# Batch 1 of the attention on the plan of batches 2 and 3, weight preparation and y's first block ahead of the second MoE

## Chip, cores and metric

The kernel runs on one core of one Trainium2 chip. The metric is the device time of one execution in microseconds (us), smaller is better.

## What is computed

```python
def _attn_ref(q, k, v, M_prev, z_prev, beta):      # B, H, S, D = 4, 8, 576, 64
    scores = scale * np.matmul(q, k.transpose(0, 1, 3, 2))
    scores = np.where(causal, -1000000000.0, scores)
    a = np.exp(scores - scores.max(-1, keepdims=True))
    a /= a.sum(-1, keepdims=True) + 1e-09
    local = np.matmul(a, v)
    mem_ret = np.einsum('bhsd,bhde->bhse', phi(q), M_prev)
    mem_norm = np.einsum('bhsd,bhd->bhs', phi(q), z_prev)[..., None] + 1e-06
    return g * mem_ret / mem_norm + (1 - g) * local

def _moe_ref(x, w_in, w_out):                      # 2304 tokens, 512 -> 2048 -> 512
    h = x @ w_in
    return (h * sigmoid(h)) @ w_out

def _moe2_ref(x, w_gate, w_val, w_out):            # 2304 tokens, 512 -> 1536 -> 512
    g = x @ w_gate
    return (g * sigmoid(g) * (x @ w_val)) @ w_out
```

The output is the second MoE of the first MoE of the attention, all in float32 (the weights of the MoEs come as float64 and are decoded on the chip).

## The kernel before, in words

Three stages follow each other. Attention and the first MoE overlap: the first MoE is cut into 256 groups of 12 matmuls (`moe1`, line 766), and the main loop at line 1203 puts attention slots between the groups. The second MoE, 36 rounds of gate and value products with the output products of earlier rounds between them, comes after.

**Precision.** A matmul on plain float32 data costs TensorE more than one on data rounded to a shorter form (`F32R`). Most operands are therefore split into a rounded high part and a rounded rest: a cast on ScalarE and a subtraction on VectorE or GpSimd, and three products (high by high, high by rest, rest by high).

**Attention** goes by units, one unit for each pair of heads (`unit`, line 306). A unit is a list of stages written as a string: `opF` for batch 1 and `opG` for batches 2 and 3 (batch 0 has two strings of its own). A "+" starts a new slot, and the next pair starts eight slots later. The two plans differ in the scores of the four 128-row blocks (`s_blk`, line 420): plan F multiplies q and k as plain float32 on 64 rows of the array for each head (line 437), plan G first splits both (`stack`, line 370: the casts of line 376, the subtractions of line 377) and makes three rounded products per head and block (line 441). Plan G also scales four of its nine attention tiles on ScalarE instead of GpSimd (line 485 GpSimd, line 489 ScalarE), and keeps one buffer for most tiles where plan F keeps two. At the start of batch 2 `open_G` closes F's tile pool and opens G's, and all slots of batch 1 end before those of batch 2 begin.

**Weights of the second MoE.** `prep_w2` (line 909) is a generator of 60 steps, 5 for each of 12 tiles of the hidden width. Each tile takes three 512 KB loads `raw` (gate, value, output: line 669 or 674), each decoded by one ScalarE and three VectorE instructions (lines 683 to 686), sums and differences for a seven-product scheme on GpSimd (lines 946 to 949), casts on ScalarE and subtractions on GpSimd (line 936), and stores to DRAM (`wg`, `wo`, line 917). It starts in `open_G`. While attention slots are left, every fifth group takes a step. Then `open_w2` (line 1016) finishes the tile under way, reloads the finished output weights from DRAM into SBUF (line 1031), and takes a step every fifth group until 24 groups are left. Then it brings in y's first block. What is left of the 60 steps is taken in the second MoE, up to three in each of its first rounds.

**y.** The first MoE's result is stored to DRAM (`yd`). `y_prep` (line 976) loads a block of 768 tokens as `ytop` and `ybot`, 768 KB each, and makes seven pieces of it, each split by a cast on ScalarE (line 993) and a subtraction on GpSimd (line 994); four of the pieces need a sum or difference first (lines 1000, 1003, 1007, 1011, VectorE). There are three blocks; twelve rounds of the second MoE use one.

**Second MoE.** A round (`up`, line 1089) makes seven products of six matmuls of 384 columns each, and between them the output products of earlier rounds (`down`, line 1165: nine matmuls of 512 columns for a tile). The last step before `down` is `pl` on GpSimd (line 1159). In this stage TensorE's order is as written; a scheduler orders all other engines, and TensorE in the first two stages. All engines execute in order, and nearly all DMAs are issued from SP's queue, also in order.

Of the kernel before, what the change touches and what calls it, by code (L numbers as in the profile page):

```python
# [25 lines left out]
    ps_m=3,  # L26
    ps_a=5,
    whi='v',
    stackb=2,
    rows=1,  # L30
    pA=0,
    sA=1,
# [18 lines left out]
    blks=1,  # L51
    pw=3,
    pt=4,
    every=5,
    late=5,
    y0=24,
    jit=3,
    G=dict(sc='ppppaaaap'),
    p_ring=15,
    pp=4,  # L60
# [31 lines left out]
def kernel(  # L92
# [15 lines left out]
    nc = tc.nc  # L108
# [69 lines left out]
    def open_at(name):  # L178
        if "x" in cur:
            cur["x"].close()  # L180
        cur["x"] = ExitStack()
        cur["pool"] = cur["x"].enter_context(tc.tile_pool(name=name, bufs=1, side="right"))
        cur["bufs"] = CFG["bufs" + name[2:]]
        cur["s4"] = [cur["pool"].tile([P, 640], F32, name=f"s4{i}") for i in range(CFG["n_s4"][name[2:]])]
        for x in cur["s4"]:
            nc.vector.memset(x[:, 576:640], 0.0)

    def open_F():
        kept.close()
        mx2.append(ph1.enter_context(tc.tile_pool(name="mx2", bufs=1)))  # L190
        open_at("atF")

    def open_G():
        open_at("atG")
        cur["pw"] = cur["x"].enter_context(tc.tile_pool(name="pw", bufs=1, side="right"))
        ph2["prep"] = prep_w2()
# [433 lines left out]
    for u, key in enumerate(units):  # L630
        step, stages = unit(u)
        if u == NP:
            stages.insert(0, lambda: open_at("atB"))
            at_slot = max(slots) + 1
        if u == 2 * NP:
            stages.insert(0, open_F)
            at_slot = max(slots) + 1
        if u == NP * CFG["stackb"] + NP:
            stages.insert(0, open_G)
            at_slot = max(slots) + 1  # L640
        for i, st in enumerate(stages):
            slots.setdefault(at_slot + i, []).append(st)
        for sup in key[2]:
            ready[key[0], sup] = at_slot + len(stages)
        at_slot += step
# [45 lines left out]
    def r_(ap):  # L691
        return ap.bitcast(F32R)
# [286 lines left out]
    def y_prep(i):  # L979
        top = ph2["yst"].tile([P, 2, T2], F32, tag="top", name="ytop")  # L980
        bot = ph2["yst"].tile([P, 2, T2], F32, tag="bot", name="ybot")
        t = ph2["yst"].tile([P, 2, HT], F32, tag="t", name="yt")
        for n, x in enumerate((top, bot)):
            nc.sync.dma_start(
                out=x, in_=yd[2 * P * n:2 * P * (n + 1), T2 * i:T2 * i + T2].rearrange("(k p) n -> p k n", p=P)
            )
        ys[i] = {}

        def put(nm, src):
            slot = (7 * i + YQ.index(nm)) % 10  # L990
            pool = ph2["yq" if slot < 7 else "ysp"]
            y = pool.tile([P, 2, 2, HT], F32, tag=f"y{slot}", name="y" + nm, bufs=1)
            nc.scalar.copy(r_(y[:, 0]), src)
            nc.gpsimd.tensor_sub(r_(y[:, 1]), src, y[:, 0])  # L994
            ys[i][nm] = r_(y)

        t0, t1, b0, b1 = top[:, :, 0:HT], top[:, :, HT:T2], bot[:, :, 0:HT], bot[:, :, HT:T2]
        yield
        put("B11", t0)
        nc.vector.tensor_sub(t, t1, t0)  # L1000
        put("T1", t)
        yield
        nc.vector.tensor_sub(t0, b1, t)
        put("T2", t0)
        yield
        put("B21", b0)
        nc.vector.tensor_sub(t1, b1, t1)
        put("T3", t1)
        yield
        put("B22", b1)  # L1010
        nc.vector.tensor_sub(t, b0, t0)
        put("T4", t)
        yield

    def open_w2():
        yield from drain()
        cur["x"].close()
        pha.close()
        ph2["wo"] = ctx.enter_context(tc.tile_pool(name="wo", bufs=1, side="right"))
        ph2["g"] = ctx.enter_context(tc.tile_pool(name="ps_g", bufs=1, space=PSUM, side="right"))  # L1020
        kept_o = list(wdo)
        x = open_prep("2", "right")
        n = 0
        while left() > CFG["y0"]:
            n += 1
            if n % CFG["late"] == 0:
                next(ph2["prep"])
            elif kept_o and n > 4:
                j = kept_o.pop(0)
                wos[j] = ph2["wo"].tile([P, 4, 256], F32, name=f"wo{j}")  # L1030
                nc.sync.dma_start(out=wos[j], in_=wdo[j])
            yield
        yield from drain()
        assert not kept_o
        x.close()
        ph2["yq"] = ctx.enter_context(tc.tile_pool(name="yq", bufs=1, side="right"))
        open_yst()
        for _ in y_prep(0):
            yield
# [143 lines left out]
    if True:  # L1183
# [16 lines left out]
        for kind, val in items:  # L1200
# [7 lines left out]
            else:  # L1208
# [10 lines left out]
                    attn_slot(slot)  # L1219
                    slot += 1  # L1220
                if slot < NSLOT:
                    if "prep" in ph2 and n_g % every == 0:
                        next(ph2["prep"], None)
                else:
                    if "late" not in ph2:
                        ph2["late"] = open_w2()
                    next(ph2["late"], None)
# [73 lines left out]
```

## Time and profile before

| what | us |
|---|---|
| median of 2 runs (lowest, highest) | 1141.92 (1141.29, 1142.55) |
| the profiled execution, device time | 1141.5 |
| its span | 1139.7 |
| TensorE busy in the span | 1097.1 (96%) |
| VectorE, ScalarE, GpSimd busy | 592.1, 519.0, 502.7 |

The span is what the profile covers; 1.8 us of the device time lie around it. Busy TensorE time is of pipelined matmuls with modelled ends, so a busy share near 100% says that TensorE hardly waited. The granted clock is TensorE's, as a share of 2.4 GHz; 0.5 is 1.2 GHz.

### The profile page before, as it was taken

How to read it: one execution, taken by the hardware profiler on the slowest of the kernel's cores; microseconds unless marked ns; L12 is line 12 of the kernel's file. 1: busy time of each engine (PE TensorE's matmuls, PEld its weight loads, DVE VectorE, ACT ScalarE, POOL GpSimd, SP SyncE). 2: the span in 40 equal slices, each digit the busy share in tenths (PEclk: the TensorE clock that was granted, in tenths of full speed). 3: DMA queues.
4: the chain of work that ended last, by engine and by line, in shares of the span. 5: the costliest groups of instructions: out<-in, count | busy, mean ns of one | idle time of the engine just before them, and what ended most of it. 6: DMA issues, size and time to landing. Idle time of an engine off the chain costs nothing.

```text
span 1139.7 us, 19219 instructions
## 1 busy us (share of the span) xinstructions
PE 1097.1 (96%) x6867; PEld 976.7 (86%) x6867; DVE 592.1 (52%) x1389; ACT 519.0 (46%) x1237; POOL 502.7 (44%) x562
## 2 busy tenths in 40 slices
PE   6899999999999999999999898799999999999998
PEld 4576877889898889989899897688989999999986
DVE  7996777765556555355635463653353333333320
ACT  6754766456555646465644343422342323323222
POOL 4675575456525426354445576641351113211123
PEclk8989999999999999999999998899999999999999
DMA  8975755455755626574449886885664645555501
GB/s 217 295 220 175 242 174 168 149 182 185 251 160 171 193 71 211 179 248 129 151 148 399 311 298 223 294 287 177 195 237 140 192 152 175 173 175 176 169 27 55
DMA packets 154479, 221.47 MB, mean 194 GB/s; under 512 B 75536, under 2 KB 108304, under 8 KB 154384
## 3 DMA queue, kind: packets, MB, share of 16 engines
q1 hardware_dynamic: 152208, 219.86, 58.7%
q8 instruction: 54, 0.88, 0.3%
q10 hardware_dynamic: 2176, 0.40, 0.2%
q14 instruction: 41, 0.34, 0.1%
HBM read 168.31 MB, written 51.90 MB: 193 GB/s over the span
## 4 chain that ended last, share of the span: by engine, by line
PE 77%; DVE 7%; POOL 5%; DMA 5%; issue 4%; ACT 2%; ACTq 0%; SPq 0%; POOLq 0%; DVEq 0%
PE y L867 16%; PE h L808 15%; PE po L1173 12%; PE gb L1104 8%; PE ga L1104 6%; PE U L576 4%; PE pst L327 3%; PE gd L1104 3%; PE gc L1104 3%; PE pss L441 2%; PE pss L437 2%; PE psm L399 1%; PE pss L471 1%; DMA raw<-in_moe_w_val_dram 1%; DVE raw L685 1%
## 5 line engine op out<-in xcount | busy, mean ns | idle before, releaser
L1159 POOL TENSOR_TENSOR pl<-r,ph 128x384 fp32r<-128x384 f32 x72 | 74.8, 1048 | 278.3 <-ACT ph L1158 217.1
L867 PE MATMUL y<-gh,w 128*128 128x320 f32 (+1 forms) x1024 | 174.9, 307 | 3.7 <-ACT gh L200 2.9
L818 POOL TENSOR_TENSOR gl<-th,gh 128x256 fp32r<-128x256 f32 (+1 forms) x128 | 110.5, 867 | 141.5 <-ACT gh L200 95.5
L808 PE MATMUL h<-xh,w 128*128 128x320 f32 (+1 forms) x1024 | 170.8, 304 | 1.2 <-ACT xh L200 0.5
L867 PEld LDWEIGHTS y<-gh,w 128*128 128x128 f32 x1024 | 147.5, 193 | 18.2 <-issue 9.3
L808 PEld LDWEIGHTS h<-xh,w 128*128 128x128 f32 x1024 | 144.6, 190 | 12.5 <-issue 7.2
L1104 PE MATMUL gb<-yT,w 128*128 128x384 f32 x648 | 134.6, 343 | 8.6 <-POOL yT L994 3.2
L1173 PE MATMUL po<-wo,ph 128*128 128x512 f32 x432 | 134.6, 397 | 3.4 <-ACT ot L1179 2.3
L1104 PEld LDWEIGHTS gb<-yT,w 128*128 128x128 f32 x648 | 118.2, 191 | 19.9 <-DVE e L1139 3.7
L816 DVE SCALAR_TENSOR_TENSOR th<-th,h 128x256 f32<-128x256 f32 (+1 forms) x128 | 57.1, 449 | 104.2 <-ACT th L815 104.0
L485 POOL TENSOR_TENSOR s<-s,r 128x128 f32<-128x128 f32 (+4 forms) x112 | 85.7, 794 | 46.4 <-DVE r L497 24.4
L1131 DVE TENSOR_TENSOR gd<-gb,e 128x384 f32<-128x384 f32 x36 | 20.4, 566 | 146.4 <-PE gb L1104 141.4
L867 PE MATMUL y<-gl,w 128*128 128x320 f32 (+1 forms) x512 | 96.0, 303 | 0.0
L808 PE MATMUL h<-xl,w 128*128 128x320 f32 (+1 forms) x512 | 93.0, 299 | 0.0
L1104 PE MATMUL ga<-yB,w 128*128 128x384 f32 x432 | 90.0, 345 | 0.6 <-issue 0.6
L1173 PEld LDWEIGHTS po<-wo,ph 128*128 128x128 f32 x432 | 79.2, 188 | 12.9 <-ACT ot L1179 3.2
L1173 PE MATMUL po<-wo,pl 128*128 128x512 f32 x216 | 85.2, 402 | 4.9 <-POOL pl L1159 4.9
L452 ACT ACTIVATE s<-s,mn 128x128 f32<-128x128 f32 (+3 forms) x128 | 71.1, 556 | 28.8 <-DVE mn L448 27.9
L1104 PEld LDWEIGHTS ga<-yB,w 128*128 128x128 f32 x432 | 79.2, 193 | 2.9 <-issue 0.9
L867 PEld LDWEIGHTS y<-gl,w 128*128 128x128 f32 x512 | 77.9, 193 | 3.1 <-issue 2.3
L815 ACT ACTIVATE th<-h 128x256 f32<-128x256 f32 (+1 forms) x128 | 51.7, 407 | 59.4 <-PE h L808 50.0
L808 PEld LDWEIGHTS h<-xl,w 128*128 128x128 f32 x512 | 76.0, 189 | 3.1 <-issue 2.4
(145 smaller groups left out, 1952.6 us busy)
## 6 DMA issues: line engine op xcount, KB each, us to landing
w<-wg SPq DMA_DIRECT2D x108, 512.0 KB, 4.3
w<-wd SPq DMA_DIRECT2D x80, 512.0 KB, 4.4
wg<-wo SPq DMA_DIRECT2D x36, 512.0 KB, 3.6
wd<-w SPq DMA_DIRECT2D x32, 512.0 KB, 3.9
raw<-in_moe_w_out_dram SPq DMA_DIRECT2D x28, 512.0 KB, 4.4
w<-wg SPq DMA_DIRECT2D x36, 256.0 KB, 3.3
raw<-in_moe_w_in_dram SPq DMA_DIRECT2D x16, 512.0 KB, 5.2
wo<-wo SPq DMA_DIRECT2D x14, 512.0 KB, 6.4
```

Source lines behind the costliest of these rows:

```text
L327: nc.tensor.matmul(dst, src, ident[0:n, 0:n], start=start, stop=True, is_transpose=True, skip_group_check=True)
L452: nc.scalar.activation(out=a, in_=a, func=ACTF.Exp, scale=-1.0, bias=mn, accum_out=o["sm", sup][:, col:col + 1])
L485: nc.gpsimd.tensor_mul(a, a, r.to_broadcast([P, w]))
L576: nc.tensor.matmul(U[64 * hh:64 * hh + 64, c0:c1], row_of("v", c)[:, hh], a(hh), start=False, stop=(m == len(todo) - 1), skip_group_check= ...
L808: nc.tensor.matmul(ps[:, :nt], w[:, kk, :], x[:, kk, :nt], start=(m == 0), stop=(m == 3 * KD - 1))
L815: nc.scalar.activation(out=th[:, :nt], in_=ps[:, :nt], func=ACTF.Tanh, scale=0.5 / WS)
L816: nc.vector.scalar_tensor_tensor(th[:, :nt], th[:, :nt], 1.0, ps[:, :nt], ALU.add, ALU.mult)
L818: tt(CFG["gl" if n >= CFG["n0"] else "gl0"]).tensor_sub(gl[:, :nt], th[:, :nt], f(gh[:, :nt]))
L867: nc.tensor.matmul(ps[:, :nt], w[:, c], g[:, :nt], start=(m == 0), stop=(m == last))
L1104: nc.tensor.matmul(dst, ws[nw][wi][:, P * kk:P * kk + P], y[ny][:, yi, kk], start=(start and m == 0), stop=(stop and m == 5), skip_group_c ...
L1159: nc.gpsimd.tensor_sub(pl, r, f(ph))
L1173: nc.tensor.matmul(po[t], a[:, c], w, start=(j == 0 and n == 0), stop=(j == F2 - 1 and n == 2))
```

## The change

Batch 1 takes plan G (`stackb=1`); G's pool is opened where F's was, so that no pool is changed between batches 1 and 2. The weight preparation exists from there on, but takes its first step at group 50 (`n_prep`), then every third group instead of every fifth, and every fourth group in `open_w2`. The reloads of the output weights take every second group. y's first block is prepared 32 groups before the end of the first MoE instead of 24, and the subtraction of y's pieces is on VectorE instead of GpSimd. In the second MoE's first rounds at most one step of preparation is taken.

```diff
@@ CFG
-    stackb=2,
+    stackb=1,
+    n_prep=50,
...
-    every=5,
-    late=5,
-    y0=24,
-    jit=3,
+    every=3,
+    late=4,
+    y0=32,
+    jit=1,
@@ def open_F():
         mx2.append(ph1.enter_context(tc.tile_pool(name="mx2", bufs=1)))
-        open_at("atF")
+        if CFG["stackb"] > 1:
+            open_at("atF")
+        else:
+            open_G()
@@ units
-        if u == NP * CFG["stackb"] + NP:
+        if CFG["stackb"] > 1 and u == NP * CFG["stackb"] + NP:
             stages.insert(0, open_G)
@@ def put(nm, src):
             nc.scalar.copy(r_(y[:, 0]), src)
-            nc.gpsimd.tensor_sub(r_(y[:, 1]), src, y[:, 0])
+            nc.vector.tensor_sub(r_(y[:, 1]), src, y[:, 0])
@@ def open_w2():
                 next(ph2["prep"])
-            elif kept_o and n > 4:
+            elif kept_o and n > 3 and n % 2 == 1:
@@ main loop
-                    if "prep" in ph2 and n_g % every == 0:
+                    if "prep" in ph2 and n_g >= CFG["n_prep"] and n_g % every == 0:
```

Lines of the changed kernel are four higher than those of before from `open_F` on.

On GpSimd at the start of the second MoE (`gl` is the last work of the first MoE, `yB` and `yT` are pieces of y, `raw` and `wo` belong to the weight preparation, `pl` to the second MoE) before:

```order
L818 TENSOR_TENSOR gl<-th,gh 128x320 x3
L994 TENSOR_TENSOR yB_8803<-ytop,yB_8803 128x768
L994 TENSOR_TENSOR yT_8807<-yt,yT_8807 128x768
L994 TENSOR_TENSOR yB_8854<-ybot,yB_8854 128x768
L994 TENSOR_TENSOR yT_8858<-ytop,yT_8858 128x768
L994 TENSOR_TENSOR yB_8881<-ybot,yB_8881 128x768
L994 TENSOR_TENSOR yT_8831<-ytop,yT_8831 128x768
L994 TENSOR_TENSOR yT_8885<-yt,yT_8885 128x768
L667 COPY raw_9176<-r 128x1
L667 COPY raw_9184<-r 128x1
L667 COPY raw_9187<-r 128x1
L1159 TENSOR_TENSOR pl<-r,ph 128x384
```

The same place now:

```order
L940 TENSOR_TENSOR wo<-t_8562,wo 128x2x256
L822 TENSOR_TENSOR gl<-th,gh 128x256 x3
L822 TENSOR_TENSOR gl<-th,gh 128x320 x4
L822 TENSOR_TENSOR gl<-th,gh 128x256 x4
L822 TENSOR_TENSOR gl<-th,gh 128x320 x4
L1163 TENSOR_TENSOR pl<-r,ph 128x384 x72
```

The seven subtractions for y's first block have left GpSimd, the last preparation stands 15 `gl` earlier, and nothing but `pl` follows to the end.

On VectorE in the last 32 groups of the first MoE (`th` and `yp` are the first MoE's two kinds of work there) now (before, `th`, `yp`, weight decoding and the four sums and differences of y's block stood there, but no `yB` or `yT`):

```order
L820 SCALAR_TENSOR_TENSOR th<-th,h 128x320 x2
L876 SCALAR_TENSOR_TENSOR yp<-y,yp 128x256 x2
L998 TENSOR_TENSOR yB_8759<-ytop,yB_8759 128x768
L876 SCALAR_TENSOR_TENSOR yp<-y,yp 128x256
L998 TENSOR_TENSOR yT_8763<-yt,yT_8763 128x768
L1007 TENSOR_TENSOR ytop<-ybot,yt 128x2x384
L998 TENSOR_TENSOR yB_8812<-ybot,yB_8812 128x768
L876 SCALAR_TENSOR_TENSOR yp<-y,yp 128x256
L998 TENSOR_TENSOR yT_8816<-ytop,yT_8816 128x768
L998 TENSOR_TENSOR yB_8833<-ybot,yB_8833 128x768
L1015 TENSOR_TENSOR yt<-ybot,ytop 128x768
L998 TENSOR_TENSOR yT_8787<-ytop,yT_8787 128x768
```

Between the last `yp` of these rows and the next `th` VectorE now has three subtractions of y's pieces and a difference to do; a `th` and a `yp` used to follow each other there.

On SP's queue where the attention has ended (`wo` with two numbers is a reload of output weights, `wo<-wo` with one a store, `raw` a load for the preparation) before:

```order
L674 DMA raw_7890<-in_moe_w_out_dram 128x1024
L712 DMA w<-wd_2_245 128x1024
L1031 DMA wo_7907<-wo_3732 128x1024
L1031 DMA wo_7932<-wo_4629 128x1024
L1031 DMA wo_7956<-wo_5567 128x1024
L712 DMA w<-wd_3_316 128x1024
L917 DMA wo_7773<-wo 128x1024
L1031 DMA wo_7980<-wo_6150 128x1024
L1031 DMA wo_8026<-wo_7075 128x1024
L1031 DMA wo_8044<-wo_7636 128x1024
L712 DMA w<-wd_4_372 128x1024
L712 DMA w<-wd_5_428 128x1024
```

And now:

```order
L1035 DMA wo_8295<-wo_6078 128x1024
L1035 DMA wo_8335<-wo_6461 128x1024
L1035 DMA wo_8373<-wo_7003 128x1024
L880 DMA yd<-yp 128x320
L1035 DMA wo_8428<-wo_7708 128x1024
L1035 DMA wo_8466<-wo_7952 128x1024
L880 DMA yd<-yp 128x320
L988 DMA ytop<-yd 128x2x768
L988 DMA ybot<-yd 128x2x768
L880 DMA yd<-yp 128x320
L673 DMA raw_8045<-in_moe_w_gate_dram 128x4x256
L673 DMA raw_8053<-in_moe_w_val_dram 128x4x256
```

Ten reloads stand together now (five more are ahead of these rows) with the loads of y's first block and of the next three `raw` right behind them; before there were seven (six in these rows), with the first MoE's own weights `w` between them, and y's loads right behind the seventh.

## Rows read from the trace of the kernel before

**Rows 1.** The page, chain that ended last, shares of the span by engine.

```profile
PE 77%; DVE 7%; POOL 5%; DMA 5%; issue 4%; ACT 2%; ACTq 0%; SPq 0%; POOLq 0%; DVEq 0%
```

**Rows 2.** Windows by stage: length, busy time of each engine (instructions), granted clock, DMA.

```profile
117.00:236.00 119.00, 119.00 (x785) 96.08 (x785) 89.18 (x247) 72.42 (x189) 70.32 (x78) 1.00 0.57 185
236.00:262.00 26.00, 24.15 (x177) 22.28 (x175) 16.39 (x37) 14.42 (x37) 16.18 (x19) 0.93 0.55 166
262.00:600.00 338.00, 337.45 (x2493) 304.79 (x2494) 182.87 (x518) 186.74 (x475) 156.48 (x206) 1.00 0.54 176
600.00:640.00 40.00, 37.10 (x262) 36.66 (x261) 18.34 (x32) 15.73 (x35) 20.73 (x22) 0.96 0.97 375
...
691.50:770.00 78.50, 64.55 (x311) 58.74 (x312) 43.63 (x61) 26.48 (x50) 43.79 (x37) 0.91 0.79 276
...
818.00:854.00 36.00, 33.83 (x167) 30.68 (x166) 18.87 (x22) 16.05 (x30) 23.74 (x15) 0.95 0.68 224
854.00:1110.00 256.00, 256.00 (x1330) 237.85 (x1328) 85.52 (x132) 73.45 (x148) 51.69 (x48) 1.00 0.48 154
```

**Rows 3.** Chain in order of time: start, length, what; rounds of the second MoE.

```profile
779.19 1.04 PE ga L1104 x6
...
788.63 1.04 PE ga L1104 x6
...
854.15 1.07 PE ga L1104 x6
...
865.72 1.07 PE ga L1104 x6
```

**Rows 4.** TensorE timeline after the first MoE: start, length, form, idle before.

```profile
690.74 0.75 PE L867 MATMUL y<-gl,w 128*128 128x320 f32 x4
...
695.46 0.97 PE L1104 MATMUL gb<-yT,w 128*128 128x384 f32 x4 [0.83 <-ACT gb L1128]
699.67 1.01 PE L1104 MATMUL gb<-yT,w 128*128 128x384 f32 x2 [3.23 <-POOL yT L994]
...
725.49 0.80 PE L1173 MATMUL po<-wo,pl 128*128 128x512 f32 x1 [2.73 <-POOL pl L1159]
...
766.98 1.31 PE L1104 MATMUL gb<-yT,w 128*128 128x384 f32 x6 [2.33 <-DVE e L1139]
```

**Rows 5.** Windows, plain float32 scores of batch 1 alone (line 437).

```profile
117.00:236.00 119.00, 21.76 (x64) 7.90 (x64) 1.00 0.57 185
```

**Rows 6.** Windows, rounded scores of batches 2 and 3 alone (line 441).

```profile
236.00:600.00 364.00, 31.16 (x192) 18.76 (x192) 1.00 0.54 176
```

**Rows 7.** Timeline, TensorE at the first scores of batch 2.

```profile
255.96 0.33 PE L441 MATMUL pss<-Kl,Qh 64*128 64x128 f32 x2 [1.85 <-POOL Kl L377]
```

**Rows 8.** Windows, the decoding of raw weights alone (line 683, one per load).

```profile
236.00:600.00 364.00, 14.15 (x21) 1.00 0.54 176
...
691.50:770.00 78.50, 3.92 (x6) 0.91 0.79 276
```

**Rows 9.** Timeline after the reloads of output weights, TensorE.

```profile
632.05 1.18 PE L867 MATMUL y<-gh,w 128*128 128x320 f32 x5 [2.88 <-ACT gh L200]
```

**Rows 10.** Lines by form: VectorE and GpSimd on two operands in SBUF.

```profile
L818 POOL TENSOR_TENSOR gl<-th,gh 128x320 fp32r<-128x320 f32 x64 | 59.1, 927 | 80.7 <-ACT gh L200 62.3 <-PE y L867 17.5 <-POOL q L202 0.5
...
L994 POOL TENSOR_TENSOR yT<-yt,yT 128x768 fp32r<-128x768 f32 x6 | 11.8, 1968 | 0.0
...
L1003 DVE TENSOR_TENSOR ytop<-ybot,yt 128x768 f32<-128x768 f32 x3 | 6.9, 2304 | 0.8 <-POOL yB L994 0.8
...
L1007 DVE TENSOR_TENSOR ytop<-ybot,ytop 128x768 f32<-128x768 f32 x3 | 3.8, 1258 | 1.1 <-DMA ybot<-yd 1.1
```

**Rows 11.** Line 1149, VectorE: shortest, median, longest in ns.

```profile
L1149 DVE SCALAR_TENSOR_TENSOR r<-sg,e x36: 549/1354/2187, 707.3 to 1105.4; 128x384 f32<-128x384 f32 x36
```

**Rows 12.** Chain in order of time, from first to second block of y.

```profile
823.19 6.37 DMA ytop<-yd
...
832.75 6.59 DMA out_dram<-ot
```

## The prediction

> **What bounds the kernel now.** I read the page's chain first: 77% of it is TensorE [rows 1], so a microsecond counts where TensorE waits, runs at the lower clock, or is spared a matmul. Then the busy time by stage [rows 2], where two columns matter: TensorE's busy time against the length of the stretch, and the granted clock. The granted clock has two levels, 1.0 (2.4 GHz) and 0.5 (1.2 GHz); a mean of 0.91 over 78.5 us means that work of 0.09 x 78.5 = 7.1 us was not done. Attention with the first MoE from 262 to 600 us is full (337.45 of 338 us, clock 1.00), and so is the second MoE after 854 us. The losses stand elsewhere: 1.85 + 1.8 us at the change of pools (236 to 262), 2.9 + 1.6 us after the end of attention (600 to 640), 14.0 + 7.1 us at the start of the second MoE (691.5 to 770), 2.2 + 1.8 us where it goes to y's second block (818 to 854) [rows 2].
>
> The second MoE can be measured more sharply by its rounds. Undisturbed, a round with y's first block takes 788.63 - 779.19 = 9.44 us, a later one 865.72 - 854.15 = 11.57 us [rows 3]; the first of all has no output products, so seven products of 1.04 us, 7.3 us. The first MoE's last matmuls end at 690.74 + 0.75 = 691.5 us [rows 4], and round 3 of the second block begins at 854.15 us: 162.7 us for 7.3 + 11 x 9.44 + 2 x 11.57 = 134.3 us of rounds. So 28.4 us are lost there. The TensorE timeline with its idle times names the causes [rows 4]: 3.23 us for GpSimd's split of y's first block, 2.73 us for `pl`, which stands behind the weight preparation on GpSimd, 2.33 us for VectorE's `e`, which stands behind the sums of y's second block, and two short waits of the 0.83 us kind on a ScalarE copy.
>
> **The change part by part.** The sum is made against the profiled execution, 1141.5 us, 0.4 us under the median of 1141.92.
>
> Scores of batch 1. The plain scores of four units keep TensorE busy for 21.76 us, 5.4 us a unit [rows 5]; the rounded ones of eight units 31.16 us, 3.9 us a unit [rows 6]. Four units save up to 6.2 us. Part of each busy time is the modelled end of a group, under which the next matmul already runs, so I take 5.0, and 3.5 as the other end. TensorE is full in batch 1 (the 21.76 us lie in a stretch with no idle time), so the saving counts. The two casts, two subtractions and the scaling that goes to ScalarE lie beside it: ScalarE and VectorE had 72.4 and 89.2 busy us in 119. **-5.0** (-6.2 to -3.5).
>
> Change of pools. The 3.7 us of 236 to 262 us hang on the empty pipeline that the new pool begins with: TensorE waited 1.85 us for the first `Kl` [rows 7]. Without the barrier between batches 1 and 2 this goes; a first `Kl` is now waited for at the start of batch 1, where GpSimd has no preparation in its queue. **-2.5** (-3.7 to 0).
>
> Start of the second MoE. All 36 raw loads (12 tiles by 3) now come before it; 6 were decoded in it [rows 8]. With them go the GpSimd queue in front of `pl`, the raw loads between the weight loads on SP, and the sums of y's second block in front of `e`, since the order brings these ahead of the stage. What is late next is the ScalarE copy (two waits, 1.4 us) and the step to y's second block, 4.0 us, with 0.5 us for the rest: 28.4 - 5.9 = 22.5 go. The bounds: nothing of the 5.9 stays, or 12 us of new waits do. **-22.5** (-28 to -11).
>
> The step to y's second block. The wait there is a chain of transfers: `ytop` for the third block lands 6.37 us after it could be issued, and an output store behind it took 6.59 us, on which `ot`'s two buffers hang [rows 12]. The order keeps store and loads in the same places. VectorE now carries four more subtractions there, in front of `gd`: **+1** (-4 to +3).
>
> Denser preparation. The attention stretch decodes 21 loads now [rows 8]; the order puts about six more into it, and all 30 come at three groups a step instead of five. Cover: VectorE is busy 182.9 us of 338, ScalarE 186.7, GpSimd 156.5 [rows 2]. By that stretch a load costs TensorE nothing; by the second MoE, where six cost some 12 us, 2 us each. I stay near the first, as it is the same stage: **+2** (0 to +12).
>
> Reloads of output weights. Ten instead of seven, then y's loads, then three raw loads: the ScalarE decode that waits for the first of these holds `th` and `gh` behind it, and TensorE waits for those, as it did for 2.88 us [rows 9]. The transfers grow by three of 512 KB, but no weights of the first MoE stand between them: **0** (-4.5, all that was lost, to +6).
>
> y's first block on VectorE. Between the `yp` and the `th` of its last groups VectorE gets seven subtractions and two differences. A subtraction of two SBUF operands of 768 took 1.26 us beside an idle GpSimd, 2.30 beside a busy one [rows 10], so nine take 11 to 21 us, with two `yp` more. TensorE has about eight groups of work ahead, 12 us. **+3** (0 to +9).
>
> The sum: -5.0 - 2.5 - 22.5 + 1 + 2 + 0 + 3 = -24.0; 1141.5 - 24.0 = 1117.5, and 0.4 for the median: 1118 us.
>
> On the subtractions the trace shows that VectorE's `r` from two SBUF operands takes 0.549 us at best and 2.187 at worst [rows 11], while nothing but GpSimd's load differs. The Trainium skill, page "SBUF — State Buffer", section "SBUF: two separate sides", says that VectorE with two SBUF inputs and GpSimd take a shared port pair by an exclusive lock, the later one waiting for the whole instruction. By that rule the move helps in the second MoE and hurts in the first, and the trace's long `r` agrees; what it would cost here is the second rival, worked out from rows.
>
> **The rivals.** The forecast, gains of 18 to 30 us, has 0.50.
>
> More comes free: the step to y's second block, reached with GpSimd idle, loses nothing (-4), the reloads spread by two groups cost nothing (-4.5): 1118 - 8.5 = 1109 us. For it: four subtractions of 1.97 us [rows 10] leave GpSimd's queue in front of `pl`. Against: the transfers of rows 12 stay. 0.14.
>
> The lock in the first MoE's tail: each of the seven subtractions waits for a `gl` of 0.93 us [rows 10], 6.5 us, and each `gl` for a subtraction, so that the tail loses 9 instead of 3 us: 1124 us. For it: rows 11. Against: TensorE's lead of eight groups. 0.15.
>
> The gain is handed back in the first MoE: the ten reloads hold the decode and cost 6 us more, preparation 6 instead of 2: 1128 us. For it: rows 9. Against: the full stretch in rows 2. 0.16.
>
> Slower: preparation every third group puts 30 loads into the attention stretch at a pace at which ScalarE, VectorE and GpSimd, all in order, hand each wait for a raw load on to TensorE. Without the +2 the sum is -26, so it decides from 26/30 = 0.87 us a load on; at 1.0 us the time is 1146 us. For it: 2 us a load in the second MoE. Against: there TensorE needed `pl` at once, here it has other groups, and 21 loads cost 0.55 us in all [rows 2]. 0.05.
>
> That the preparation isn't out of the second MoE after all is excluded by the order: every raw load stands ahead of the first `wg` load.
>
> **How the numbers follow.** About 2% (22.8 us, 1119.1 us) is what a measurement of this kernel can tell from no change. The forecast lies 1 us under that line: of its 0.50 I put 0.37 under it, all of the 0.14, and 0.02 of the two middle rivals: faster 0.53. Slower by over 2% (1164.8 us) takes 1.7 us a load: 0.02. The rest, 0.45, is within 2%. The range from 1106 to 1131 us leaves out the slower rival and the outer tenth or so of the others.
>
> **What would show it.** Right: no raw decode after the first `ga` product; the first rounds at 9.44 us but for two short copy waits; line 441 at about 46 us for twelve units, line 437 gone from batch 1; a window across the start of batch 2 with full TensorE and clock 1.00. Wrong: rounds of the first block over 10 us; TensorE idle behind `th` or `gh` in the last 32 groups (y on VectorE) or some 15 us after attention's end (reloads); busy TensorE time in the attention stretch more than 3 us under its length (density).

## The result, and the profile after

The changed kernel takes 1109.45 us (median of two runs, 1108.69 to 1110.22) against 1141.92 before: 0.9729 of it, with a 95% interval of 0.9701 to 0.9757. That is 32.5 us less, where 24 were forecast; it lies in the range, 8.5 us under the likeliest value. The profiled execution has a span of 1106.9 us, 32.8 less than the 1139.7 of before.

The page's chain, which answers to [rows 1]: TensorE's share went from 77% to 86%, GpSimd's from 5 to 2%, DMA's from 5 to 2%.

```profile
PE 86%; DVE 6%; ACT 2%; DMA 2%; POOL 2%; issue 2%; SPq 0%; ACTq 0%; DVEq 0%; POOLq 0%
```

Windows by stage, as in [rows 2] (length, busy time of TensorE, its weight loads, VectorE, ScalarE and GpSimd with instructions, granted clock, DMA share and rate); the steps between stages and the second MoE move with the kernel, while 262 to 600 and 600 to 640 us are the same times as before; what follows attention is counted separately below, since attention now ends earlier.

```profile
117.00:229.00 112.00, 112.00 (x823) 97.90 (x822) 94.59 (x255) 84.60 (x217) 62.90 (x69) 1.00 0.63 200
229.00:262.00 33.00, 32.45 (x237) 27.40 (x235) 25.45 (x66) 21.99 (x58) 24.29 (x29) 1.00 0.64 213
262.00:600.00 338.00, 337.50 (x2484) 304.75 (x2483) 198.70 (x522) 191.36 (x484) 182.01 (x235) 1.00 0.68 228
600.00:640.00 40.00, 38.92 (x292) 38.45 (x292) 21.91 (x37) 18.95 (x45) 30.43 (x34) 1.00 0.88 309
680.90:757.00 76.10, 74.72 (x405) 70.40 (x405) 27.40 (x51) 18.50 (x39) 7.14 (x7) 1.00 0.67 218
785.00:821.00 36.00, 33.25 (x172) 30.11 (x171) 24.32 (x31) 16.27 (x30) 10.49 (x8) 1.00 0.66 232
821.00:1077.00 256.00, 256.00 (x1330) 238.04 (x1329) 88.41 (x136) 73.24 (x147) 44.15 (x44) 1.00 0.49 154
```

Read the TensorE time against the length, and the clock. At the start of the second MoE 74.72 of 76.10 us are busy at 1.00, where 64.55 of 78.5 were at 0.91, and GpSimd there is down from 43.79 to 7.14 us: the preparation has gone. ScalarE's last decode of a raw weight starts at 625.5 us, and none follows. The clock is 1.00 in each of these stages; every fall that [rows 2] show is gone. Attention with the first MoE is as full as before, 337.50 of 338 us, although GpSimd does 25.5 us more in it. What stays is 2.75 us at the step to y's second block.

The TensorE timeline with its idle times, as in [rows 4]: the end of the first MoE, the two copy waits that were foreseen, and the step to y's second block.

```profile
681.16 0.75 PE L871 MATMUL y<-gl,w 128*128 128x320 f32 x4
...
683.96 1.31 PE L1108 MATMUL gb<-yT,w 128*128 128x384 f32 x6 [0.83 <-ACT gb L1132]
...
693.20 1.31 PE L1108 MATMUL gb<-yT,w 128*128 128x384 f32 x6 [0.55 <-ACT gb L1132]
...
797.49 0.73 PE L1177 MATMUL po<-wo,ph 128*128 128x512 f32 x2 [0.67 <-ACT ph L1162]
798.94 0.50 PE L1177 MATMUL po<-wo,pl 128*128 128x512 f32 x1 [0.71 <-POOL pl L1163]
...
803.61 1.32 PE L1108 MATMUL gb<-yT,w 128*128 128x384 f32 x6 [1.37 <-DVE gd L1135]
```

The waits of 3.23, 2.73 and 2.33 us are gone. The loss by rounds, counted as before: the last `y` matmuls end at 681.9 us, one `ga` product of 1.05 us already stands between them, so 680.9 to 821.40 us are 140.5 us for 134.3 us of rounds. 6.2 us are lost instead of 28.4.

The chain in order of time at that step, as in [rows 12] (start, length, what) shows why `gd` is late: not the output store, which no longer stands in it, but VectorE's queue. (`gd` and `e` are sums of products that VectorE makes; the next `gb` products wait for them.)

```profile
789.73 5.10 DMA ytop<-yd
794.85 0.96 DVE yt L1004
...
798.05 1.65 DVE ytop L1007
...
801.31 1.77 DVE yt L1015
803.08 0.49 DVE gd L1135
...
809.83 1.07 PE ga L1108 x6
...
821.40 1.07 PE ga L1108 x6
```

These `ytop` and `yt` belong to y's *third* block, which is not used for another 130 us: the order issues its loads as soon as the buffer is free, and its sums stand in front of `gd`.

Three rows divide the whole time. They are the first and last start of a form of matmul: the last `U` is attention's end, the last `y` the first MoE's, and `gc` (one product a round) runs through the second MoE. The kernel before, lines by tile (count, duration in ns as shortest/median/longest, first and last start):

```profile
L576 PE MATMUL U<-tb,v_t x320: 219/432/484, 74.3 to 578.5; 128*64 128x320 f32 x96, 128*64 128x192 f32 x32, 128*64 128x64 f32 x32
...
L1104 PE MATMUL gc<-yT,w x216: 334/336/522, 693.3 to 1098.3; 128*128 128x384 f32 x108
```

And the changed kernel, the same view:

```profile
L580 PE MATMUL U<-tb,v_t x320: 219/432/484, 75.3 to 571.7; 128*64 128x320 f32 x96, 128*64 128x192 f32 x32, 128*64 128x64 f32 x32
...
L1108 PE MATMUL gc<-yT,w x216: 333/336/339, 681.7 to 1065.5; 128*128 128x384 f32 x108
```

Attention ends 6.8 us earlier, the second MoE begins 11.6 us earlier (693.3 to 681.7), and from its first to its last `gc` it takes 383.8 instead of 405.0 us, 21.2 less. 11.6 + 21.2 = 32.8, the whole gain of the span.

### The profile page after: what moved, and what is told of

It is laid out like the page before. It is cut to its first block, busy times and chain, and to the rows that moved or that the text cites. A ratio compares the mean times of both kernels' runs of the same rounds, so it can differ in the third digit from the quotient of the medians.

```text
span 1106.9 us, 19317 instructions
## 1 busy us (share of the span) xinstructions
PE 1080.7 (98%) x6899; PEld 969.0 (88%) x6899; DVE 609.9 (55%) x1412; ACT 525.4 (47%) x1261; POOL 451.1 (41%) x529
## 4 chain that ended last, share of the span: by engine, by line
PE 86%; DVE 6%; ACT 2%; DMA 2%; POOL 2%; issue 2%; SPq 0%; ACTq 0%; DVEq 0%; POOLq 0%
PE y L871 17%; PE h L812 17%; PE po L1177 13%; PE gb L1108 10%; PE ga L1108 6%; PE U L580 4%; PE pss L445 3%; PE pst L331 3%; PE gd L1108 3%; PE gc L1108 3%; PE psm L403 1%; PE pss L475 1%; DVE raw L689 1%; PE U L331 1%; DVE raw L690 1%
## 5 line engine op out<-in xcount | busy, mean ns | idle before, releaser
L822 POOL TENSOR_TENSOR gl<-th,gh 128x256 fp32r<-128x256 f32 (+1 forms) x128 | 114.3, 898 | 130.4 <-ACT gh L204 79.5
L1108 PE MATMUL gb<-yT,w 128*128 128x384 f32 x648 | 131.8, 338 | 2.8 <-ACT gb L1132 1.4
L489 POOL TENSOR_TENSOR s<-s,r 128x128 f32<-128x128 f32 (+4 forms) x96 | 70.8, 765 | 57.8 <-DVE r L501 32.7
L1108 PE MATMUL ga<-yB,w 128*128 128x384 f32 x432 | 87.2, 337 | 0.0
L1108 PEld LDWEIGHTS ga<-yB,w 128*128 128x128 f32 x432 | 76.8, 188 | 2.1
L1162 ACT CAST ph<-r 128x384 fp32r<-128x384 f32 x72 | 36.2, 514 | 88.9 <-PE po L1177 57.1
```

Source lines behind the costliest of these rows:

```text
L489: nc.gpsimd.tensor_mul(a, a, r.to_broadcast([P, w]))
L822: tt(CFG["gl" if n >= CFG["n0"] else "gl0"]).tensor_sub(gl[:, :nt], th[:, :nt], f(gh[:, :nt]))
L1108: nc.tensor.matmul(dst, ws[nw][wi][:, P * kk:P * kk + P], y[ny][:, yi, kk], start=(start and m == 0), stop=(stop and m == 5), skip_group_c ...
L1162: nc.scalar.copy(ph, r)
```

## The experiments

The ledger theory is that of the prediction: each part has a price of its own, and most of the gain is the clear start of the second MoE. Its rivals: the plan of batch 1 is the main cause (plan theory), or y's subtractions leaving GpSimd (contention theory). Times are medians, beside runs of the kernel before on the same chip.

**The plan alone.** The kernel before, with `stackb=1`, and preparation from the group at which it began before:

```diff
-    stackb=2,
+    stackb=1,
+    n_prep=53,
```

> The kernel before with batch 1 on the plan of batches 2 and 3 and nothing else: preparation begins at the same group as before and runs every fifth group, y's first block stays late and on GpSimd. Ledger theory (most of the 32 us comes from the start of the second MoE): only the scores (5.0) and the change of pools (2.5) go, 1142 - 7.5 = 1134 us (1131 to 1137), line 441 at about 46 us for twelve units, and the second MoE still loses about 28 us. Plan theory (the plan of batch 1, with the pipeline kept full and the clock kept high, is the main cause): 1122 us or less. Contention theory (y's subtractions leaving GpSimd are the main cause): 1134 us as well, it is told apart by the third kernel.

1129.7 against 1140.7 us, ratio 0.9901 (0.9880 to 0.9923): 11.0 us (8.8 to 13.7), more than 7.5 and far less than 20. The second MoE begins at 681.1 us, 12.2 earlier, and is nearly as long as before (402.9 us by its `gc`):

```profile
L1108 PE MATMUL gc<-yT,w x216: 334/336/338, 681.1 to 1084.0; 128*128 128x384 f32 x108
```

Attention ends at 567.9 us in it by the same kind of row as above, 10.6 earlier than before.

**Everything but the plan.** The changed kernel with

```diff
-    stackb=1,
+    stackb=2,
```

> The changed kernel with batch 1 on its old plan, the pools changed again between batches 1 and 2; preparation dense, y early and on VectorE. Ledger theory: 7 to 8 us of the 32 are lost, 1117 us (1115 to 1119), the change of pools costs 3.7 us again and line 437 has 64 instructions again; the second MoE's rounds are as in the changed kernel. Plan theory: 1130 us or more. Contention theory: 1117 us as well.

1138.1 against 1140.7 us, ratio 0.9975 (0.9960 to 0.9990): it keeps 2.6 of the 32 us. The plan theory had this figure and not the one before it; the ledger missed this one by 21 us and stood at the edge of its bounds with the other (gains of 5 to 11 us). 11.0 and 2.6 make 13.6, not 32: the parts are worth more together than apart. The rows of this kernel say where:

```profile
L580 PE MATMUL U<-tb,v_t x320: 219/432/796, 74.4 to 591.9; 128*64 128x320 f32 x96, 128*64 128x192 f32 x32, 128*64 128x64 f32 x32
...
L1108 PE MATMUL gc<-yT,w x216: 334/336/338, 711.6 to 1095.4; 128*128 128x384 f32 x108
```

The second MoE is as short as in the changed kernel, 383.8 us. Its whole gain is there, and it is paid back in front: attention ends 13.4 us later than before, and the second MoE begins 18.3 us later. Dense preparation is cheap in the changed kernel and dear in this one.

**y's subtractions back on GpSimd.**

```diff
-            nc.vector.tensor_sub(r_(y[:, 1]), src, y[:, 0])
+            nc.gpsimd.tensor_sub(r_(y[:, 1]), src, y[:, 0])
```

> The changed kernel with the twenty-one subtractions of y back on GpSimd. Ledger theory: the start of the second MoE is clear of preparation all the same, so only a wait for GpSimd's split of y's first block (3.2 us before) and up to 2 us at the step to y's second block come back: 1113 us (1110 to 1116). Contention theory: the waits for pl and for y come back, 15 us or more, 1125 us. Lock theory (a VectorE operation with two SBUF inputs waits for whole GpSimd instructions, so the move costs in the first MoE's tail): 1106 us, faster than the changed kernel.

1109.8 against 1140.7 us, ratio 0.9727 (0.9713 to 0.9742): the same as the changed kernel, to what can be measured. Contention and lock theory both fall, and the ledger's 1113 us is too much. Two small things cancel in part: the first MoE's last `y` starts at 683.9 instead of 681.6 us, and the round at the step to y's second block takes 13.98 instead of 15.12 us (the distance between two rounds' `gc`). The profiled spans are 1108.5 and 1106.9 us.

**The old spacing of the preparation.**

```diff
-    every=3,
-    late=4,
+    every=5,
+    late=5,
...
-    jit=1,
+    jit=3,
```

> The changed kernel with the old spacing of the weight preparation (every fifth group, every fifth in the tail, three steps a round in the second MoE): nine raw loads instead of none fall into the second MoE. Ledger theory: 2 us a load, 18 us, 1127 us (1120 to 1135), with waits for pl behind GpSimd and a mean granted clock under 1.00 there. Contention theory: with y's subtractions off GpSimd the loads cost little, 1111 us (1109 to 1114). Plan theory: 1110 us.

1125.6 against 1140.7 us, ratio 0.9867 (0.9851 to 0.9884): 15.1 of the 32 us stay. As the ledger theory has it. In the TensorE timeline the waits for `pl` are back:

```profile
704.99 0.80 PE L1177 MATMUL po<-wo,pl 128*128 128x512 f32 x1 [2.25 <-POOL pl L1163]
...
719.38 0.50 PE L1177 MATMUL po<-wo,pl 128*128 128x512 f32 x1 [1.54 <-POOL pl L1163]
```

and the second MoE takes 400.0 us, 16.2 more for nine loads, 1.8 us a load, where 2 were estimated:

```profile
L1108 PE MATMUL gc<-yT,w x216: 334/336/338, 680.2 to 1080.2; 128*128 128x384 f32 x108
```

The subtractions of y's pieces are on VectorE here, so it is the preparation itself that `pl` waits behind.

**The change of pools put back.** Why is dense preparation dear without the new plan? In the first runs' traces the loss starts where the pools change. There attention's pipeline is empty, since the new pools wait for the old ones, and the unit plan has to be refilled stage by stage. This kernel has the new plan and the dense preparation, and only the change of pools between batches 1 and 2 (eight more slots) in addition:

```diff
-            open_G()
+            open_at("atG")
...
-        if CFG["stackb"] > 1 and u == NP * CFG["stackb"] + NP:
+        if u == 3 * NP:
             stages.insert(0, open_G)
```

The changed kernel ran beside it once more:

> The changed kernel once more, beside the next three on one chip: 0.973 of the time before, 1109 to 1110 us, which all theories expect; the others are measured against it.

1108.4 against 1140.1 us, ratio 0.9720 (0.9706 to 0.9735).

> The changed kernel, plan and spacing of preparation kept, but the attention's pools closed and opened again between batches 1 and 2 as before. Ledger theory (each part has its own price): the change of pools alone comes back, 2.5 to 3.7 us, 1113 us. Refill theory (formed after the first runs: behind the change of pools attention's pipeline is empty, TensorE has only the first MoE's groups, and dense preparation in front of th and Kl on VectorE and GpSimd is waited for directly): 15 us or more, 1125 us or above, with TensorE idle behind th near 255 us and the end of attention 10 us later. Scores theory (the plain scores of batch 1 are what makes the dense preparation dear): 1113 us, since they don't come back.

1128.1 against 1140.1 us, ratio 0.9894 (0.9867 to 0.9922): 19.6 us lost, as the refill theory has it. The ledger's 2.5 to 3.7 us is out by far, and so is the scores theory. Again the second MoE is 383.8 us long, and only its start moves, from 681.7 to 702.3 us:

```profile
L580 PE MATMUL U<-tb,v_t x320: 219/432/484, 74.0 to 582.9; 128*64 128x320 f32 x96, 128*64 128x192 f32 x32, 128*64 128x64 f32 x32
...
L1108 PE MATMUL gc<-yT,w x216: 334/336/338, 702.3 to 1086.1; 128*128 128x384 f32 x108
```

The timeline of all engines at the refill of this kernel (start, length, engine, form, idle before):

```profile
245.39 0.67 ACT L687 ACTIVATE t<-raw 128x512 f32<-128x512 f32 x1 [0.99 <-DMA raw<-in_moe_w_gate_dram]
...
247.14 1.05 POOL L951 TENSOR_TENSOR S<-S,t 128x256 f32<-128x256 f32 x1
...
248.16 1.44 POOL L381 TENSOR_TENSOR Kl<-K,Kh 128x512 fp32r<-128x512 f32 x1
248.51 1.63 DVE L689 SCALAR_TENSOR_TENSOR t<-raw,t 128x512 int32<-128x512 int32 x1
...
249.65 0.33 PE L445 MATMUL pss<-Kl,Qh 64*128 64x128 f32 x2 [1.50 <-POOL Kl L381]
...
251.27 0.47 DVE L820 SCALAR_TENSOR_TENSOR th<-th,h 128x320 f32<-128x320 f32 x1
...
251.81 1.17 PE L871 MATMUL y<-gh,w 128*128 128x320 f32 x3 [1.02 <-DVE th L820]
```

GpSimd makes the preparation's `S` before `Kl`, and VectorE decodes `t` for 1.63 us before `th`; TensorE's next matmuls need them, so it waits for both, and the clock is at half for some 7 us from 250 us on. Attention ends 11.2 us later than in the changed kernel. About half of that stands at the refill: from 236 to 300 us TensorE is idle for 2.95 us instead of 0.55, at a mean clock of 0.95 instead of 1.00, 5.6 us in all. From 300 us to attention's end it is idle for another 4.4 us instead of 0.4.

The rest of the 20.6 us, 9.4, is lost between attention's end and the second MoE: TensorE waits there 3.80 us for `th` and 2.58 us for `gh`, with seven decodes in that stretch instead of six. The longer wait is again one behind the preparation, now on ScalarE, whose casts of `wo` wait for VectorE's decode and stand in front of `th`:

```profile
618.64 0.62 ACT L204 CAST wo<-t 128x512 fp32r<-128x512 f32 x1 [2.90 <-DVE t L690]
...
620.55 0.38 ACT L819 ACTIVATE th<-h 128x256 f32<-128x256 f32 x1
...
621.51 1.63 PE L812 MATMUL h<-xh,w 128*128 128x320 f32 x8 [3.80 <-DVE th L820]
```

**Preparation from behind the refill.** The same kernel with

```diff
-    n_prep=50,
+    n_prep=62,
```

> The changed kernel with the change of pools between batches 1 and 2 put back, as in the run that lost 19.6 us, and the preparation beginning nine groups later, behind the refill of attention's pipeline. Refill theory (dense preparation costs because it stands in front of th and Kl while the pipeline refills): the end of attention comes 5 us or more earlier than 582.7 us and the time falls to 1122 us or less. Squeeze theory (the eight slots that the change of pools adds squeeze attention's stages into fewer groups each, and dense preparation is dear all along): 1125 to 1130 us, the end of attention at 580 us or later.

1125.2 against 1140.1 us, ratio 0.9857 (0.9841 to 0.9874). Attention's end says refill, the time says squeeze:

```profile
L580 PE MATMUL U<-tb,v_t x320: 219/432/484, 74.1 to 572.3; 128*64 128x320 f32 x96, 128*64 128x192 f32 x32, 128*64 128x64 f32 x32
...
L871 PE MATMUL y<-gl,w x512: 277/308/549, 65.5 to 697.4; 128*128 128x256 f32 x86, 128*128 128x320 f32 x85
```

The last `U` starts at 572.3 instead of 582.9 us, 0.6 us from the changed kernel: with the preparation behind the refill, the loss in attention is gone, although only one load fewer is decoded in attention (28 instead of 29). But the loads that begin nine groups later must go somewhere, and the stretch behind attention (eight decodes, last `U` to last `y`) is now 125.1 us long, 15.2 more than in the changed kernel. TensorE waits there again, as the list of its waits from 572.3 to 698 us shows (waited for: us in total, times, longest):

```profile
PE y L871 <- ACT gh L204: 6.2, 3, 4.4
PE y L871 <- DMA w<-wd: 3.9, 1, 3.9
PE h L812 <- DVE yp L876: 2.4, 1, 2.4
```

So the refill theory is borne out for attention, and not for the time: of the 19.6 us some 3 come back, and the rest is lost in another place. The number of decodes doesn't explain that place: with the old spacing eight of them stood in a stretch of 112.0 us. Why the waits behind attention come with the change of pools is not settled.

**The scores alone.** The first experiment with the change of pools put back in the same way (old spacing, y late and on GpSimd):

```diff
-            open_G()
+            open_at("atG")
...
-        if CFG["stackb"] > 1 and u == NP * CFG["stackb"] + NP:
+        if u == 3 * NP:
```

> The kernel before with batch 1 on the plan of batches 2 and 3, but with the pools closed and opened again between batches 1 and 2 as before: the scores alone. With the old sparse preparation the plan without the change of pools gave 11.3 us. Ledger theory: scores 5.0 us, 1135.5 us against 1140.5 before, so that the change of pools cost 6 us even at the old spacing. Rival: the change of pools costs its visible 2.5 to 3.7 us at the old spacing and the scores save 7.5 to 9 us: 1132 us.

1133.7 against 1140.1 us, ratio 0.9938 (0.9917 to 0.9959): 6.4 us (4.7 to 9.5), between the two expectations. The pools' change at the old spacing is then worth 11.0 - 6.4 = 4.6 us, and with both intervals anything from 1 to 8; by the start of the second MoE (687.2 and 681.1 us) it is 6.1. At the new spacing it is 19.6.

**y's first block late.**

```diff
-    y0=32,
+    y0=24,
```

> The changed kernel with y's first block brought in 24 groups before the end of the first MoE instead of 32. Ledger theory: the block's split is on VectorE and short (0.96 us a piece), so it is late by at most the 3.2 us that TensorE waited for it before, 1111 us (1109 to 1113). Contention theory (y's early block is a main part of the gain): 1115 us or more.

1108.2 against 1140.1 us, ratio 0.9720 (0.9705 to 0.9734), level with the changed kernel and below the ledger's bounds. On VectorE the block is in time either way; bringing it forward has no measurable value.

**The reloads at the old condition.**

```diff
-            elif kept_o and n > 3 and n % 2 == 1:
+            elif kept_o and n > 4:
```

> The changed kernel with the reloads of the output weights at the old condition (every group from the fifth that has no preparation, instead of every second from the fourth). If spreading the reloads gave the 3.4 us that the stretch behind attention gained, 1112 us (1111 to 1113), with TensorE idle behind th or gh near 605 us; if that gain came from elsewhere, 1108.5 to 1109 us.

1110.2 against 1140.1 us, ratio 0.9732 (0.9718 to 0.9747), not separable from the changed kernel's 0.9720. In the traces the stretch from the last `U` to the last `y` is the same to 0.1 us (572.6 to 682.4, and 571.6 to 681.4 in the changed kernel's second run). The spread reloads gave nothing there.

**y's third block held back.** To free VectorE at the step to y's second block, the loads of the third wait for an `r` of the second block:

```diff
         for n, x in enumerate((top, bot)):
+            if i > 1:
+                nc.gpsimd.tensor_copy(x[:, 0, 0:1], f(gate[-2]))
             nc.sync.dma_start(
```

> The changed kernel with y's third block held back: its loads wait for an r of the second block's ninth round, so that its sums no longer stand in front of gd on VectorE at the step to y's second block. If that step's loss (3.55 us: a round of 15.12 instead of 11.57) is VectorE's queue, the round falls to 11.6 to 12.5 us and the time by 2.5 to 3.5 us, to 1106 us against the changed kernel's 1109.5. If it is the transfers or the output store, the round stays at about 15 us and the time at 1109 to 1110 us. If the held block is late in turn, the loss appears at the step to the third block instead.

1107.9 against 1140.1 us, ratio 0.9714 (0.9699 to 0.9729). The round at the step falls from 15.11 to 11.90 us, as VectorE's queue would have it. The edit takes the third block's transfers away from the step as well, but in the changed kernel none of TensorE's waits there is for a transfer: 0.67 us for `ph`, 0.71 for `pl`, 1.37 for `gd`, and all three are gone here. GpSimd's four `pl` take 3.91 us instead of 6.41. But 2.2 us come back in the second block's tenth round (13.75 us), two rounds before the third block is used, in this kernel's timeline of VectorE and of TensorE:

```profile
903.42 0.96 DVE L1006 TENSOR_TENSOR yt<-ytop 128x768 f32<-128x768 f32 x1 [5.26 <-DMA ytop<-yd]
...
905.17 0.56 DVE L1137 TENSOR_TENSOR gd<-gb,e 128x384 f32<-128x384 f32 x1
...
905.78 0.45 PE L1110 MATMUL gb<-yT,w 128*128 128x384 f32 x1 [1.20 <-DVE gd L1137]
```

VectorE stands at `yt`, which waits for its transfer, with `gd` behind it. So the loads were let go three rounds earlier, and `yt` and the first copy were held instead:

```diff
         yield
+        if i > 1:
+            nc.gpsimd.tensor_copy(t[:, 0, 0:1], f(gate[-2]))
         put("B11", t0)
...
+            if i > 1 and nm == "B11":
+                nc.gpsimd.tensor_copy(r_(y[:, 0, 0, 0:1]), f(gate[-2]))
             nc.scalar.copy(r_(y[:, 0]), src)
...
-                    if j == 8:
+                    if j == (5 if i else 8):
...
-                    if j in (8, 9, 10):
+                    if j in (5 if i else 8, 9, 10):
```

> The changed kernel with y's third block held as before (its loads now wait for an r of the second block's sixth round) and its first sum and first copy held for an r of the tenth round, so that VectorE doesn't wait for the transfer with gd behind it. If the 2.2 us that the first version lost at the step to the third block were that wait, both steps run at 11.6 to 12.0 us a round and the time is 1105.5 us; if the block is then late for gb, the step to the third block takes 13 us or more and the time is 1107 us or above.

1105.8 against 1140.1 us, ratio 0.9696 (0.9680 to 0.9711): the fastest version here. Both rounds now run clear, 11.91 and 11.57 us. At the first of them VectorE's `gd` waits for TensorE, and no longer the other way round:

```profile
800.04 0.57 DVE L1141 TENSOR_TENSOR gd<-gb,e 128x384 f32<-128x384 f32 x1 [3.70 <-PE gb L1114]
```

Its interval and that of the changed kernel beside the first held version (0.9706 to 0.9735) overlap by a little, so the 2.7 us between their medians rest on the rounds, whose 3.2 us the trace shows.

## Why the prediction was right, and where not

The direction, the place of most of the gain, and the likeliest mechanism were right; the size was 8.5 us short, and one idea behind the sum was wrong. By place, on the spans: up to attention's end 5.5 us were forecast and 6.8 gained, behind it 3 were to be lost and 3.8 were gained, at the start of the second MoE 21.5 were forecast and 22.2 gained. So most of what was missed lies behind attention.

**The start of the second MoE (-22.5, and +1 for the step).** Right: 28.4 us of loss became 6.2, a gain of 22.2 where the two terms made 21.5. No raw decode starts after 625.5 us, the two copy waits of 0.83 and 0.55 us are there, and from the third round on the first block's rounds run at 9.43 to 9.49 us. The price per load holds too (1.8 us in the run with old spacing). At the step to y's second block the size was near (3.55 us lost, where 4.0 and 1 more were expected) and the reason wrong: I put it on the transfers of [rows 12], and the chain and the held block show VectorE's queue. That the four subtractions on VectorE cost about 1 us there, as the term said, the run with GpSimd confirms: 13.98 against 15.12 us.

**The scores (-5.0).** 6.4 us in the run with the scores alone, just past the far end of my bounds; its interval of 4.7 to 9.5 us doesn't exclude the 5.0. The busy time says more than 5.0, so I may have taken off too much for modelled ends; that is not shown. Windows of line 445, the rounded scores of all twelve units in the changed kernel, which answer to [rows 5, 6]:

```profile
117.00:236.00 119.00, 16.29 (x111) 10.35 (x111) 1.00 0.63 202
236.00:600.00 364.00, 27.92 (x177) 16.44 (x177) 1.00 0.67 226
```

44.21 us for twelve units are 3.7 us a unit, 14.7 for batch 1, and 21.76 - 14.7 = 7.0 us.

**The change of pools (-2.5) and the denser preparation (+2).** Here the ledger itself was wrong. I priced the change of pools by the idle time that [rows 7] show, and the density by the stretch behind it, each as if the other were not there. Apart, the first is worth some 4.6 us, and the second, with the rest of the change but the plan, loses 18.3 us ahead of the second MoE for the 21.2 that it brings there; with dense preparation the change of pools costs 19.6 us. Taken together in this kernel, attention ends 3.8 us later than with the plan alone (571.7 and 567.9 us), which is what the +2 stood for. That the sum came out here is partly luck: the change does both at once. For the changed kernel with the pools changed as before, the ledger's price of 2.5 to 3.7 us would have been wrong by 16 to 17 us. I also miscounted the density: six more loads were to come into the attention stretch, by [rows 8], whose window goes on to 600 us. Up to the last `U` there are 19 before and 30 after, behind it 11 and 6, in the second MoE 6 and none.

**The reloads (0) and y's first block on VectorE (+3).** Between attention's end and the second MoE [rows 4] and the `U` row give 691.5 - 578.5 = 113.0 us before, and 680.9 - 571.7 = 109.2 after: 3.8 us gained where 3 were to be lost, the largest miss. The wait of 2.88 us for `gh` [rows 9] and the half clock behind it are gone. The spread reloads are not the reason (the run with the old condition), nor is y's place in time. With the old spacing `h` waited there again, for 3.1 us behind a decode on VectorE, with eight decodes behind attention; so it is the spacing that counts, which leaves six there instead of eleven. That the smaller number alone does it is not shown. The subtractions on VectorE cost next to nothing: all waits of TensorE in that stretch are 1.1 us. For the seven and two differences in the first MoE's tail I had feared 11 to 21 us of VectorE time; one row of line 998 gives all of one form, shortest, median and longest in ns:

```profile
L998 DVE TENSOR_TENSOR yT<-ytop,yT x6: 945/959/1305, 646.6 to 929.0; 128x768 fp32r<-128x768 f32 x6
```

0.96 us as a rule and 1.31 at the longest. The 1.26 us that I read in [rows 10] as the time beside an idle GpSimd is a mean of 0.95, 1.02 and 1.80. In the tail GpSimd is seldom at work just beside them. Its timeline in that stretch:

```profile
639.67 0.88 POOL L822 TENSOR_TENSOR gl<-th,gh 128x320 fp32r<-128x320 f32 x1 [0.61 <-ACT gh L204]
645.64 1.44 POOL L822 TENSOR_TENSOR gl<-th,gh 128x320 fp32r<-128x320 f32 x1 [5.09 <-ACT gh L204]
651.47 1.43 POOL L822 TENSOR_TENSOR gl<-th,gh 128x320 fp32r<-128x320 f32 x1 [4.39 <-ACT gh L204]
```

Where a `gl` and a subtraction meet, both grow (0.88 to 1.44 us at 645.64, and the subtraction that VectorE begins at 646.59 takes 1.30; a sum of the same size at 676.87, beside the `gl` of 676.26, takes 1.63), but GpSimd stands idle for 4 to 5 us between them, here waiting for ScalarE. By the rule of the Trainium skill, page "SBUF — State Buffer", section "SBUF: two separate sides", VectorE with two SBUF inputs and GpSimd exclude each other for a whole instruction; the meetings agree with it. The rival at 1124 us charged every subtraction with a `gl`, and the step that failed is that count of meetings. On GpSimd the same work takes 1.83 to 2.57 us, and the tail is 2.7 us longer (571.3 to 683.9 against 571.7 to 681.6).

**The rivals.** "More comes free" had the nearest time, 1109 us, by the wrong way: it had 4 us at the step to y's second block, where the changed kernel gained next to nothing, and 4.5 us at the reloads, where 3.8 came, but with the spacing of the preparation. The two rivals of the first MoE's tail and the slower one did not happen in this kernel. The mechanism of the slower one, dense preparation handing its waits on to TensorE, is real: the runs with the change of pools show it. (Its chance of a loss over 2% was given from 1.7 us a load on; the sum gives 1.6.)

## What to carry to other kernels

A point where a pipeline is emptied and refilled can cost more than the idle time seen there, above all with dense side work (1.85 us seen; 4.6 beside the sparse preparation, 19.6 beside the dense one): remove it first, then pack the side work tighter, and try the two together as well as apart. Moving the side work out of its way may only move the loss, as the run with the later start did. Work that an order issues as soon as its buffer is free can stand in front of work that is needed now on an engine that runs in order; hold it by a dependence on a later result, the transfer early and the first reader late. Split the time at a few fixed instructions (last of one stage, first of the next), for then a gain in one stage and its loss in another show at once.

## What the runs showed of the hardware that was not expected

- How much VectorE and GpSimd slow each other hangs on whether their instructions meet, and not on the load over a stretch: behind attention, with GpSimd busy for 49.04 of 110.30 us, 16 of VectorE's 18 operations of 128x768 took 0.94 to 0.96 us, and two that met a `gl` 1.30 and 1.63. At the step to y's second block, where GpSimd makes four `pl` in a row (797.52 to 803.93 us), sums of that size took 1.65 and 1.77.
- Of VectorE's `r`, only those with both operands in SBUF were slowed. Line 1149 of the kernel before makes `r` from `sg` and `e`, both in SBUF, in 549 to 2187 ns [rows 11]. From `sg` and `gb`, which lies in PSUM, the same line takes, as shortest, median and longest:

```profile
L1149 DVE SCALAR_TENSOR_TENSOR r<-sg,gb x36: 540/543/557, 706.8 to 1106.0; 128x384 f32<-128x384 f32 x36
```

- The clock held at 1.00 through the waits of 0.83 and 1.37 us in the second MoE of the changed kernel; before, those of 1.85, 2.73, 2.88 and 3.23 us were each followed by a stretch at half clock, that of 2.33 us was not. The waits that stay here cost only themselves, and with the long ones their stretches at half clock went too.
